# Half a tile of features: both parts of w1 in one stationary operand, and the gate logits on VectorE

## The chip, the core and the metric

The kernel runs on one core of a Trainium2 chip. The metric is the device time of one execution in microseconds, median of several runs. TensorE (PE) multiplies a stationary operand of up to 128 columns with a moving one and adds into PSUM; VectorE (DVE), ScalarE (ACT) and GpSimd (POOL) work element by element; SyncE (SP) issues nearly all transfers between the memories.

## The reference

Two branches of the same input `x` (2048 tokens, 640 features) are mixed by a gate. Branch A is a long convolution over the tokens, whose taps come from a state-space model; branch B is a feed-forward layer with 1728 hidden features.

```python
x = A_u                                               # (1, 2048, 640)
g = sigmoid((x * gate_w).sum(-1, keepdims=True))      # one logit per token
a = conv(x, K) + x * D_skip                           # K: taps, 2048 for each of 640 channels
b = relu(x @ w1) @ w2                                 # w1 (640, 1728), w2 (1728, 640)
return g * a + (1 - g) * b
```

where `K = 2 Re sum_n C[d,n] exp(A[d,n] dt[d] l)` for l = 0 to 2047 (128 terms for each channel).

## The kernel before

**Precision by parts.** Every operand of the feed-forward layer is split into a high part in a rounded 32-bit format (`F32R`) and a low part, the rest: `xh`, `xl` of the tokens, `w1h`, `w1l`, `w2h`, `w2l` of the weights, `hh`, `hl` of the hidden values. A product is the sum of three matmuls, high by high, high by low, low by high. ScalarE makes the high part by a copy, VectorE the low part by a subtraction.

**Tiling.** The 2048 tokens are 8 groups (`g`) of 256. The 1728 hidden features are 13 tiles of 128 and one of 64, the half tile. `PARTS = (5, 5, 4)` deals them to three passes (`p`) over the groups; the half tile is the first of pass 0 (`f = 0`). Its stationary operand has 128 columns: 64 features, then the gate weights as column 64, then zeros. So row 64 of its product is the gate logit of each token.

- `weights` (in `feed_forward`) loads a tile of w1 (`wq` in pass 0, `ws` later) or w2 (`ws`) and splits it.
- `load_x` loads a group's tokens into `xs`, a ring of one buffer. `trans` transposes them on TensorE in three thirds (banks `pk`, `px`, `pg` for group 0, `pk` alone for the others) and splits them into `xh`, `xl`; `store` puts both in `xt`, from which passes 1 and 2 reload them.
- `hidden` makes two tiles of hidden features in one PSUM bank (`pf`, two banks): 3 matmuls of 256 columns for each of 5 blocks `k` of input features and each tile. `high` (ReLU on ScalarE) and `low` (VectorE) make `hh` and `hl` of both. For the half tile, `zc` copies row 64 to `z`, and `zs` stores it to memory.
- `sums` makes the output of a group in four pieces `j` of 128 tokens by 320 columns: 3 matmuls for each hidden tile. In pass 0 ScalarE copies the result to `q`, later passes add with VectorE; `part` holds the sums between passes.
- `gates`, at the start of pass 1, loads all logits and makes `gate` and `omg` (1 - gate) by 17 small VectorE steps.
- `params` computes the parameters of the taps, a chain of VectorE and ScalarE steps on 128 x 640 tiles in the first 80 us, among them an absolute value (`ac`, `as`), reciprocals, arctangent and square root, each of the last two behind a load of ScalarE's tables. The rows that result (`hl` of `split`) are stored to `ps`.
- `ssm` generates the taps in 40 chunks of 16 channels: `load_rows` loads 8 chunks' rows (`PS`, two buffers), `phases` and `exponents` make arguments on TensorE (`pg`, `px`, `pe`), ScalarE makes exponentials and sines, `factors` multiplies on VectorE (`G`, `mg`, `cs`, `sn`), `taps` sums on TensorE (`pk`) and stores to `kd`.
- `conv` is a transform of 64 by 32 points in five blocks of 128 channels: `stage1`, `stage2`, `inv2`, `relay`, `inv1`. Its TensorE work (`pc`) alternates with passes 1 and 2 of the feed-forward layer. The output is mixed as it comes (`with_y`, `with_last`, `inv1`).

**The order.** All these are tasks of a planner (`Plan`): each has an engine, a queue, a duration as its author estimates it, a rank, and what it needs of ring buffers. Tasks of one queue stay in order. When the program is built the planner goes through the time by these estimates and writes a fixed order of instructions for each engine, which the engines then follow. So a change of any duration or dependence can move work between engines everywhere. Generator tasks have a better rank on TensorE than the feed-forward layer's, which fills what they leave.

All instructions go through a helper, so the profile puts nearly all on line 228; groups are told apart by their tiles.

Of the kernel before, what the change touches and what calls it, by code (L numbers as in the profile page):

```python
# [19 lines left out]
NT = D // 128  # L20
# [4 lines left out]
SPIN = 10  # L25

# [223 lines left out]
class Kernel:  # L250
    def __init__(self, tc, ctx, io, out):
# [8 lines left out]
                       xt=[T([2, 128, NT, 256], f"xt{g}") for g in range(8)], z=T([16, 128], "z_"),  # L260
# [17 lines left out]
    def feed_forward(self):  # L278
# [4 lines left out]
        for n, k in dict(ws=3, wq=5, xs=1, xhl=2, q=2, bank=2, z=1).items():  # L283
            ring(n, k)
# [49 lines left out]
        def load_x(g, after=()):  # L334
            s_ = tok('xs')

            def load():
                st['xs', g] = self.xp.tile([128, 2, D], F32, name="xs")
                for h in range(2):
                    D_.dma_start(st['xs', g][64 * h:64 * h + 64], xd[h, :, 2 * g:2 * g + 2, :])  # L340
            return s_, A('SP', 'x', 1.25, load, after, take=[s_], kb=640, rank=2 if g else 0)

        def trans(g, third, src):
# [34 lines left out]
            if third == 2:  # L378
                xst[g] = A('SP', 'st', 1.25, store, X[0, g], use=[x_], kb=1280, rank=6)
# [15 lines left out]

        def hidden(p, g, i, fs):
            b_, h_ = tok('bank'), tok(f"h{i}")

            def pe(r, f, third):
                def go():  # L400
# [3 lines left out]
                    wh, wl = (w.rearrange("p (k f) -> p k f", f=128) for w in (wh, wl))  # L404
                    for k in range(2 * third, min(2 * third + 2, NT)):
                        for m, (a, b) in enumerate(((wh, xh), (wh, xl), (wl, xh))):
                            self.E.matmul(st['hb'][:, r], a[:, k], b[:, k], start=k == m == 0,
                                          stop=k == NT - 1 and m == 2)
                return go
            ts = []  # L410
            for r, f in enumerate(fs):
                (wt, w_) = W[p, f, 0]
                for third in range(3):
                    x = X[p, g] if p else X[p, g][2 * third:2 * third + 2]
                    new = r == third == 0
                    ts.append(A('PE', 'ff', 0.72 if third < 2 else 0.36, pe(r, f, third), [*wt, *x],
                                take=[b_] if new else (), use=[w_, xtok[p, g]] + ([] if new else [b_]), mode='f'))

            if p == 0 and i == 0:
                z_ = tok('z')  # L420

                def zc():
                    st['z'] = pa.tile([65, 256], F32, name="z")
                    V.tensor_copy(st['z'][64:65], st['hb', i][64:65, 0])

                def zs():
                    D_.dma_start(sc['z'][2 * g:2 * g + 2], st['z'][64:65].rearrange("o (t p) -> o t p", t=2))
                zt = A('DVE', 'ff', 0.36, zc, ts, take=[z_], use=[b_], rank=0)
                self.zst.append(A('SP', 'st', 0.62, zs, [zt], use=[z_], kb=2, rank=6))

            def high():
                st['h', i] = [pa.tile([128, len(fs), 256], F32R, name=f"h{x}{i}") for x in 'hl']
                S.activation(st['h', i][0], st['hb', i][:, :len(fs)], AF.Relu)

            def low():
                V.scalar_tensor_tensor(st['h', i][1], st['hb', i][:, :len(fs)], 0.0, st['h', i][0].bitcast(F32),
# [800 lines left out]
```

## Time and profile before

| | |
|---|---|
| median of 3 runs | 714.4 us (713.83 to 715.64) |
| profiled execution: time, span | 717.8 us, 716.0 us |
| mean granted TensorE clock | 0.986 |
| busy: TensorE, VectorE, ScalarE, GpSimd | 679.6, 575.4, 389.2, 72.2 us |
| moved by transfers | 110.84 MB, 155 GB/s |
| first matmul of the generator (`pg`) | 105.08 us |
| first matmul of the convolution (`pc`) | 434.15 us |

A row of a group gives the line, the engine, the operation, output and input tiles, shapes, the count, the busy time, the mean of one in ns, and the idle time before it with what ended it. A row of the timeline gives start and length in us; where rows follow one another they are merged and counted. The chain of waits is followed back from the last instruction.

### The profile page before, as it was taken

The page shows a single profiled execution, that of the slowest core. Times are in us where ns is not written, and L with a number is a line of the kernel's source. Part 1 is how long each engine was busy: PE and PEld are TensorE (multiplying, and loading weights), DVE is VectorE, ACT ScalarE, POOL GpSimd, SP SyncE. Part 2 cuts the span into 40 slices and gives each one's busy share as a digit, 9 for nine tenths or more (in the row PEclk, how much of TensorE's full clock was granted, in tenths as well). Part 3 has the DMA queues.
Part 4 walks back from the last instruction along what each step waited for, and adds up shares of the span by engine and source line. Part 5 has one row for each costly group of instructions (what it writes and reads, how often), then busy time and mean ns, then how long its engine had stood idle before and what let it go on. Part 6 is the DMA issues. An engine that isn't in the chain of part 4 may idle for free.

```text
span 716.0 us, 21643 instructions
## 1 busy us (share of the span) xinstructions
PE 679.6 (95%) x9489; PEld 600.1 (84%) x9489; DVE 575.4 (80%) x833; ACT 389.2 (54%) x572; POOL 72.2 (10%) x81
## 2 busy tenths in 40 slices
PE   5979999999999999999999999989999999899897
PEld 5979998898999999989998897886587776597695
DVE  4499628988999999999999986649869769479675
ACT  4353339999998778787889820151340531241330
POOL 1000002211121221112211100000000000010020
PEclk9899999999999999999999999999999999899999
DMA  9844773254467334423432759924915914731534
GB/s 219 242 193 163 260 240 111 67 179 163 138 199 248 125 124 139 160 88 103 153 108 89 226 166 303 270 93 137 199 44 170 251 56 119 177 97 61 120 98 96
DMA packets 92167, 110.84 MB, mean 155 GB/s; under 512 B 30945, under 2 KB 73705, under 8 KB 91817
## 3 DMA queue, kind: packets, MB, share of 16 engines
q1 hardware_dynamic: 91992, 109.38, 51.9%
q8 instruction: 74, 1.21, 0.7%
q14 instruction: 21, 0.16, 0.1%
q10 hardware_dynamic: 80, 0.08, 0.0%
HBM read 70.24 MB, written 39.20 MB: 153 GB/s over the span
## 4 chain that ended last, share of the span: by engine, by line
PE 69%; DVE 14%; ACT 10%; issue 4%; DMA 2%; SPq 1%; DVEq 0%; ACTq 0%
PE pf L228 40%; PE pc L228 21%; PE pk L228 4%; DVE sn L228 3%; ACT cs L228 3%; DVE G L228 2%; DVE mg L228 2%; ACT sn L228 2%; PE pg L228 2%; ACT L228 1%; PE px L228 1%; DMA xs<-in_A_u_dram 1%; SPq L228 1%; ACT hh L228 1%; DVE cs L228 1%
## 5 line engine op out<-in xcount | busy, mean ns | idle before, releaser
L228 PE MATMUL pf<-xh,w1h 128*128 128x256 f32 x560 | 165.0, 295 | 0.6 <-ACT xh L228 0.6
L228 PE MATMUL pf<-xl,w1h 128*128 128x256 f32 x560 | 159.9, 286 | 0.6 <-DVE xl L228 0.6
L228 PE MATMUL pf<-xh,w1l 128*128 128x256 f32 x560 | 159.5, 285 | 0.0
L228 PE MATMUL pf<-w2h,hh 128*128 128x320 f32 x448 | 140.0, 315 | 2.8 <-DVE hl L228 2.0
L228 PE MATMUL pf<-w2l,hh 128*128 128x320 f32 x448 | 137.6, 310 | 0.0
L228 PEld LDWEIGHTS pf<-xh,w1h 128*128 128x128 f32 x560 | 108.5, 194 | 22.9 <-issue 20.0
L228 PE MATMUL pf<-w2h,hl 128*128 128x320 f32 x448 | 126.4, 311 | 0.5 <-DVE hl L228 0.5
L228 ACT ACTIVATE hh<-pf 128x512 fp32r<-128x512 f32 (+1 forms) x64 | 34.7, 543 | 149.3 <-PE pf L228 142.4
L228 PEld LDWEIGHTS pf<-xl,w1h 128*128 128x128 f32 x560 | 108.5, 194 | 1.8 <-DVE xl L228 0.8
L228 PEld LDWEIGHTS pf<-xh,w1l 128*128 128x128 f32 x560 | 108.5, 194 | 0.0
L228 DVE TENSOR_TENSOR t<-pc,kw 128x512 f32<-128x512 f32 x80 | 53.9, 691 | 50.3 <-ACT kw L228 50.2
L228 PEld LDWEIGHTS pf<-w2h,hh 128*128 128x128 f32 x448 | 84.1, 188 | 11.6 <-issue 5.9
L228 PEld LDWEIGHTS pf<-w2l,hh 128*128 128x128 f32 x448 | 84.2, 188 | 2.4 <-issue 1.6
L228 PEld LDWEIGHTS pf<-w2h,hl 128*128 128x128 f32 x448 | 80.8, 188 | 6.3 <-issue 4.6
L228 POOL TENSOR_TENSOR me<-me,cm 128x512 f32<-128x512 f32 x40 | 51.5, 1287 | 192.7 <-DVE cs L228 115.2
L228 DVE TENSOR_TENSOR mg<-mg,cs 128x1024 f32<-128x1024 f32 x40 | 56.4, 1409 | 1.3
L228 PE MATMUL pc<-va,tm 64*64 64x128 f32 x1280 | 55.3, 277 | 1.9 <-issue 1.9
L228 DVE TENSOR_TENSOR sn<-pg,cs 128x1024 f32<-128x1024 f32 x40 | 48.7, 1216 | 8.6 <-ACT cs L228 8.3
L228 ACT ACT_TABLE_LOAD x42 | 53.9, 1283 | 0.7
L228 ACT CAST cs<-pg 128x1024 int32<-128x1024 f32 x40 | 40.4, 1011 | 20.0 <-PE pg L228 19.8
L228 DVE STREAM_TRANSPOSE vk<-va 128x512 f32<-128x512 f32 x40 | 46.9, 1233 | 4.2 <-ACT va L228 4.2
L228 DVE SCALAR_TENSOR_TENSOR hl<-pf,hh 128x512 fp32r<-128x512 f32 (+1 forms) x64 | 39.3, 616 | 12.3 <-ACT hh L228 11.8
(140 smaller groups left out, 1218.9 us busy)
## 6 DMA issues: line engine op xcount, KB each, us to landing
part<-q SPq DMA_DIRECT2D x16, 640.0 KB, 3.8
xh<-xt SPq DMA_DIRECT2D x16, 640.0 KB, 4.5
xl<-xt SPq DMA_DIRECT2D x16, 640.0 KB, 7.1
q<-part SPq DMA_DIRECT2D x16, 640.0 KB, 4.0
ws<-in_B_w_dram SPq DMA_DIRECT2D x22, 320.0 KB, 3.9
xs<-in_A_u_dram SPq DMA_DIRECT2D x16, 320.0 KB, 4.0
xt<-xh SPq DMA_DIRECT2D x8, 640.0 KB
xt<-xl SPq DMA_DIRECT2D x8, 640.0 KB
```

Of the source, the lines that this page charges most:

```text
L228: return lambda *a, **k: self._tc.keep_in_program_order(f(*a, **k))
```

## The change

In pass 0 the half tile's stationary operand now holds the high part of its 64 features in columns 0 to 63 and the low part in columns 64 to 127. Two matmuls per block, with `xh` and with `xl`, give all the products, in two halves of the PSUM tile that have to be added: ScalarE copies the upper half to `z` (`fold`), VectorE adds the lower one (`total`), ScalarE makes the high part of the hidden values in rows 0 to 63 (`half_high`), VectorE the low part in rows 64 to 127 of the same tile (`half_low`). w2's 64 rows are loaded twice, one copy below the other, so that two matmuls, with `w2h` and `w2l`, do for the three of before.

The gate logits leave TensorE: `gw` holds the gate weights on all 128 partitions, and for each of 16 blocks of 128 tokens one VectorE instruction multiplies `xs` by it in place and adds up the row into `z`, after the group's transposes are through. The next `load_x` waits for both of a group's logits. The logit's way through memory (`zc`, `zs`, the load in `gates`) goes, as do the two memsets. `PS` holds 4 chunks' rows instead of 8. Some names in `conv` get a further index.

```diff
+XS = 1
 ...
+        self.z = keep.tile([128, 16], F32, name="logit")
 ...
         def weights(p, f, two, after=()):
-            first = p == 0 and not two
+            first, half = p == 0 and not two, fn < 128 and not two
 ...
                 if two:
-                    if fn < 128:
-                        P.memset(t[fn:], 0.0)
-                    D_.dma_start(t[:fn], io['B_w2'][f0:f0 + fn, :])
+                    for x in range(0, 128, fn):
+                        D_.dma_start(t[x:x + fn], io['B_w2'][f0:f0 + fn, :])
                     return
                 t = t.rearrange("p (k f) -> p k f", f=128)
-                if fn < 128:
-                    P.memset(t[:, :, fn + 1:], 0.0)
                 D_.dma_start(t[:, :, :fn], io['B_w1'][:, f0:f0 + fn].rearrange("(k p) f -> p k f", p=128))
-                if fn < 128:
-                    D_.dma_start(t[:, :, fn:fn + 1], io['gate_w'].rearrange("(k p o) -> p k o", p=128, o=1))
 ...
             def high():
+                if half:
+                    w, t = (x.rearrange("p (k f) -> p k f", f=128) for x in (st[key][0], st['ws', key]))
+                    S.copy(w[:, :, :fn], t[:, :, :fn])
+                    return
 ...
             def low():
+                if half:
+                    w, t = (x.rearrange("p (k f) -> p k f", f=128) for x in (st[key][0], st.pop(('ws', key))))
+                    V.tensor_sub(w[:, :, fn:], t[:, :, :fn], w[:, :, :fn].bitcast(F32))
+                    return
 ...
+        def logits(g):
+            s_, ld = xs[g]
+
+            def go(t):
+                x = st['xs', g][:, t]
+                V.scalar_tensor_tensor(x, x, 1.0, self.gw, op0=ALU.mult, op1=ALU.mult,
+                                       accum_out=self.z[:, 2 * g + t:2 * g + t + 1])
+            for t in range(2):
+                self.zs.append(A('DVE', 'z', 0.75, lambda t=t: go(t), [*self.x_read[-3:], self.gwl], use=[s_], rank=0))
 ...
         def hidden(p, g, i, fs):
+                    ms = ((wh, xh), (wh, xl), (wl, xh))[:2 if halves(p, f) else 3]
 ...
+            n = len(fs) - halves(p, fs[0])
+            lo = len(fs) - n
+
+            def fold():
+                st['z'] = pa.tile([64, 256], F32, name="z")
+                S.copy(st['z'], st['hb', i][64:, 0])
+
+            def total():
+                V.tensor_add(st['z'], st['hb', i][:64, 0], st['z'])
 ...
+            def half_high():
+                S.activation(st['h', i][0][:64, 0], st['z'], AF.Relu)
+
+            def half_low():
+                h = st['h', i][0][:, 0]
+                V.scalar_tensor_tensor(h[64:], st['z'], 0.0, h[:64].bitcast(F32), op0=ALU.max, op1=ALU.subtract)
 ...
+                x = A('ACT', 'ff', 0.32, fold, ts, take=[z_], use=[b_], rank=0)
+                x = A('DVE', 'ff', 0.35, total, [x], use=[b_, z_], rank=0)
+                x = A('ACT', 'ff', 0.32, half_high, [x, a], use=[z_, h_], rank=0)
+                x = A('DVE', 'ff', 0.35, half_low, [x], use=[z_, h_], rank=0)
 ...
         def sums(p, g, j, q_, qld):
-            prod = [(f, *x) for f in range(n) for x in ((0, 0), (0, 1), (1, 0))]
+            prod = [(f, *x) for f in range(n) for x in ((0, 0), (0, 1), (1, 0))[:2 if halves(p, f) else 3]]
 ...
+        def load_gate():
+            D_.dma_start(self.gw, io['gate_w'].rearrange("(o d) -> o d", o=1).to_broadcast([128, D]))
         xs = {0: load_x(0)}
         W[0, 0, 0] = weights(0, 0, 0)
+        self.gwl = A('SP', 'w', 0.62, load_gate, kb=320, rank=1)
 ...
         def load_rows(c):
-                t = gk.tile([128, 8, 128], F32R, name="PS", bufs=2)
-                src = self.sc['ps'][c > 0][c // 8 - 1 if c else 0]
+                t = gk.tile([128, 4, 128], F32R, name="PS", bufs=2)
+                src = self.sc['ps'][c >= 8][c // 8 - (c >= 8), c % 8 * C:c % 8 * C + 4 * C]
```

More of the change, by code (lines that the diff above doesn't have):

```diff
@@ L415, in hidden @@
                     new = r == third == 0
-                    ts.append(A('PE', 'ff', 0.72 if third < 2 else 0.36, pe(r, f, third), [*wt, *x],
+                    ts.append(A('PE', 'ff', (0.72 if third < 2 else 0.36) * (2 / 3 if halves(p, f) else 1), pe(r, f, third), [*wt, *x],
                                 take=[b_] if new else (), use=[w_, xtok[p, g]] + ([] if new else [b_]), mode='f'))
[L419 to L429, printed above, removed]
+            n = len(fs) - halves(p, fs[0])
@@ new lines, in half_high @@
+            def half_high():
[3 more added lines that the diff above has]
+                V.scalar_tensor_tensor(h[64:], st['z'], 0.0, h[:64].bitcast(F32), op0=ALU.max, op1=ALU.subtract)
+            a = A('ACT', 'ff', 0.12 + 0.2 * n, high, ts, take=[h_], use=[b_], rank=0)
+            b = A('DVE', 'ff', 0.08 + 0.27 * n, low, [a], use=[b_, h_], rank=0)
+            H[p, g, i] = [(a, b)] * len(fs), h_
@@ L540, in go @@
                 V.tensor_mul(self.omg, z, self.gate)
-            a = A('SP', 'q', 0.62, load, self.zst, kb=8, rank=3)
-            rec = Recorder(V)
+            rec, a = Recorder(V), self.zs
             for k in range(17):
-                a = A('DVE', 'gate', 0.2, rec.one(k, 17, go), [a], rank=4)
-            self.gated = a
-        self.zst, self.x_read = [], []
+                a = [A('DVE', 'gate', 0.2, rec.one(k, 17, go), a, rank=4)]
+            self.gated = a[0]
+        self.zs, self.x_read = [], []
         def spin():
```

70 lines of the change are left out of this document (36 added, 34 removed).

## The prediction

> **What bounds the kernel now.** I read the page's busy shares and chain first, then the busy times in three stretches, then the rows around each wait of TensorE.
>
> ```profile
> PE 679.6 (95%) x9489; PEld 600.1 (84%) x9489; DVE 575.4 (80%) x833; ACT 389.2 (54%) x572; POOL 72.2 (10%) x81
> ...
> PE 69%; DVE 14%; ACT 10%; issue 4%; DMA 2%; SPq 1%; DVEq 0%; ACTq 0%
> ```
>
> TensorE is busy for 95% of the span and carries 69% of the chain, so work taken from it counts unless something else comes last in its place. The three stretches (core's PE, PEld, DVE, ACT, POOL busy, clock, DMA share, GB/s) are: before the generator of the convolution taps starts, the generator, and the convolution.
>
> ```profile
> 0.00:105.00 105.00, 91.76 (x655) 90.44 (x656) 64.25 (x120) 39.36 (x72) 1.81 (x9) 0.95 0.74 224
> 105.00:434.00 329.00, 320.81 (x4479) 301.43 (x4477) 303.55 (x420) 271.68 (x325) 60.22 (x60) 1.00 0.45 144
> 434.00:716.00 282.00, 267.07 (x4360) 208.21 (x4358) 207.64 (x293) 78.20 (x176) 10.15 (x12) 0.98 0.54 142
> ```
>
> TensorE idles 13.2 us in the first stretch, 8.2 in the second, 14.9 in the third. VectorE is loose first (40.8 idle), but in the second it is nearly as full as TensorE (25.4 idle of 329). So the change exchanges TensorE time against VectorE time where VectorE has least to spare.
>
> **What leaves TensorE.** A row of a matmul shows its length with the pipeline in it; the cost is the spacing, which two pieces of the chain show: 15 hidden matmuls of 256 columns, and 60 output matmuls of 320.
>
> ```profile
> 89.63 1.79 PE pf L228 x15
> 91.70 8.81 PE pf L228 x60
> ```
>
> That is 0.119 us and 0.147 us each. In the half tile each of 8 token groups loses 5 hidden matmuls (three per k become two, five k) and 4 output matmuls (three products become two in each of four sums). The built instruction order agrees: 1680 hidden and 1344 output matmuls become 1640 and 1312. 40 x 0.119 + 32 x 0.147 = 9.5 us. That the change doesn't do what it says is thereby ruled out. The Trainium skill (TensorE: Matmul & The Clock Gate, Back-to-back issue gap) gives an isolated warm gap of N/2.4 + 2.5 ns; by it the removed work would be an estimated 8.7 us. The trace's spacings are some 10 ns wider than that, and they decide.
>
> **What VectorE and ScalarE get.**
>
> ```profile
> L228 DVE SCALAR_TENSOR_TENSOR sa<-sa,ra 128x640 f32<-128x640 f32 x6 | 4.9, 820 | 0.1
> L228 DVE SCALAR_TENSOR_TENSOR hl<-pf,hh 128x512 fp32r<-128x512 f32 x48 | 32.8, 683 | 10.8 <-ACT hh L228 10.3
> L228 DVE SCALAR_TENSOR_TENSOR hl<-pf,hh 128x256 fp32r<-128x256 f32 x16 | 6.6, 415 | 1.4 <-ACT hh L228 1.4
> L228 DVE TENSOR_TENSOR xl<-pk,xh 128x256 fp32r<-128x256 f32 x7 | 2.9, 412 | 0.0
> L228 DVE COPY z<-pf 1x256 f32<-1x256 f32 x8 | 3.4, 422 | 16.6 <-PE pf L228 15.0 <-ACT hh L228 1.6
> L228 ACT ACTIVATE hh<-pf 128x512 fp32r<-128x512 f32 x48 | 28.6, 596 | 142.7 <-PE pf L228 135.8 <-DVE z L228 6.8
> L228 ACT ACTIVATE hh<-pf 128x256 fp32r<-128x256 f32 x16 | 6.1, 383 | 6.6 <-PE pf L228 6.6
> ```
>
> Per group VectorE gains two logits (0.82 each: the 128x640 instruction of the same kind), the add of the two halves (0.41) and the low part of the half (0.42); it loses the copy of the logit row (0.42) and half of one low part (0.27): +1.78, or 14.2 us over 8 groups. No row has a logit's accumulating output: 0.82 is the lower bound, two passes (1.64) the upper; I take 0.82, since two full-width f32 inputs already cost no more in that row. ScalarE gains two 64x256 steps (0.38 each) and loses 0.21: +0.55 per group, 4.4 us, in 327 us of its own idle time. Five groups' VectorE work lies at least partly ahead of 105 us, where it is loose; three groups (5.3 us) fall into the full stretch.
>
> The removed logit transfers, the two memsets on GpSimd and the smaller gate load had nobody waiting long; the row loads become ten of half the size, each buffer still freed four chunks (some 33 us, 329/40 x 4) before its next use: nothing for all of these.
>
> **First wait: the second token load.** Its buffer is the only one, and the logits now hold it longer.
>
> ```profile
> 9.06 1.11 SPq L228 DMA_DIRECT2D xs<-in_A_u_dram  x2
> 10.05 0.41 DVE L228 TENSOR_TENSOR xl<-pg,xh 128x256 fp32r<-128x256 f32 x1
> 17.99 1.08 PE L228 MATMUL pk<-ident,xs 128*128 128x128 f32 x4 [4.67 <-DMA xs<-in_A_u_dram]
> ...
> xs<-in_A_u_dram SPq DMA_DIRECT2D x16, 320.0 KB, 4.0
> ```
>
> The load was issued at 9.06, as soon as the transposes were through. In the new order both logits stand behind the last xl; its weight step is 0.4 shorter, so they end near 10.05 + 2 x 0.82 = 11.7. The load then lands between 11.7 + 0.6 + 4.0 = 16.3 (the usual landing) and 11.7 + 8.9 = 20.6 (as slowly as now, where weights share the queue). Ahead of it on SP there are now 480 KB more (gate weights on all partitions, the half's w2 twice), 2.2 us at 224 GB/s, against a column load that goes. I take 1.3 us later (0 to 2.7). The first group's five hidden matmuls lie ahead of this wait, so their 0.6 us brings nothing.
>
> **Second wait: the parameter chain.**
>
> ```profile
> 32.09 0.74 ACT L228 ACTIVATE ac<-ld_A_C_real 128x640 f32<-128x640 f32 x1
> 33.49 0.83 DVE L228 TENSOR_TENSOR mx<-ac,as 128x640 f32<-128x640 f32 x1 [3.48 <-ACT as L228]
> 33.97 0.43 ACT L228 COPY q<-pf 128x320 f32<-128x320 f32 x1 [0.51 <-PE pf L228]
> 39.72 0.82 DVE L228 TENSOR_TENSOR r<-mn,s 128x640 f32<-128x640 f32 x1
> 47.87 0.63 DVE L228 TENSOR_TENSOR xl<-pk,xh 128x512 fp32r<-128x512 f32 x1
> 48.55 1.12 PE L228 MATMUL pk<-ident,xs 128*128 128x128 f32 x4 [4.80 <-DVE xl L228]
> ```
>
> TensorE waits here for xl, which stands behind ScalarE's arctan steps. In the new order `ac` comes after the third q copy, not the second: 34.40 + 1.3 - 3 x 0.147 = 35.3, and with the 1.4 from ac to mx, mx starts near 36.6, 3.1 late. Up to r, VectorE has three steps of the half tile more (1.24): r ends near 44.9 instead of 40.54. Then arctan and square (1.5), with one table load less ahead of xh than before, and seven of the chain's VectorE steps: xl ends near 49.5, 1.05 later than now. Without it TensorE would come here 0.1 late (1.3 less the 0.59 of four output and 0.6 of five hidden matmuls). The wait grows by 0.95 (0 to 2).
>
> **Four smaller costs, behind that.**
>
> ```profile
> 85.00 0.60 PE L228 MATMUL pk<-ident,xs 128*128 128x128 f32 x4
> 86.95 0.68 DVE L228 TENSOR_TENSOR xl<-pk,xh 128x512 fp32r<-128x512 f32 x1
> 89.03 0.60 PE L228 MATMUL pk<-ident,xs 128*128 128x128 f32 x4
> ```
>
> *The transpose bank.* xl is through at 87.63, and TensorE wants the bank at 89.03: 1.4 us of slack. Now xh queues behind the half's second ScalarE step, which needs the fold, the add and their order in one PSUM bank: about 0.8 longer, more with a chain step of 0.8 between. 0 to 0.5 in each of six groups: 0.7 in sum (0 to 3).
>
> ```profile
> 80.87 0.82 DVE L228 TENSOR_TENSOR hl<-ld_A_log_A_real,hl 128x640 fp32r<-128x640 f32 x1
> 82.75 5.75 SPq L228 DMA_DIRECT2D ps<-hl  x6
> 94.05 2.73 SPq L228 DMA_DIRECT2D PS<-ps  x2
> 105.08 0.63 PE L228 MATMUL pg<-tg,PS 128*128 128x512 f32 x2
> ```
>
> *The generator's start.* The chain's last VectorE step, at 81.7, comes up to 3.1 + 1.2 + 4 x 0.82 = 7.6 us later, less what goes into its own waits: some 6. The six stores, issued by 88.5, then end near 95, and behind a token load and two stores of x the row loads are issued near 98. TensorE now gets there at 105.1 + 1.05 - 3.5 (what groups 1 to 4 save after the wait) = 102.6, and 98 + 4 to 6 is when the rows land: 0.6 (0 to 3).
>
> *VectorE in the generator.* 5.3 us go into 25.4 of idle time. TensorE always has hidden and output work to go on with there, but in a fixed order: 0.7 (0 to 5.3).
>
> *The convolution.* Behind its first instruction the new order has 399 hidden and 336 output matmuls instead of 420 and 338. These 2.8 us of filling are missing in two of its five blocks, and TensorE already idles 14.9 us there: 0.9 of it isn't gained (0 to 2.8).
>
> **The sum.** -9.5 + 0.6 + 1.3 + 0.95 = -6.65, then + 0.7 + 0.6 + 0.7 + 0.9 = -3.75. The profiled execution took 717.8 us (span 716.0, 1.8 around it), 3.4 above the median of 714.4; the difference is carried over: 717.8 - 3.75 = 714.05 there, **710.7 in the median**. Its own range is 708 to 713.
>
> **Rivals.** A measurement tells this kernel from no change at about 0.3%, 2.1 us: faster is under 712.3, slower over 716.5.
>
> *All is gained* (0.16): the four smaller costs and the second wait come to nothing: -9.5 + 0.6 + 1.3 = -7.6, 706.8. For it: TensorE idles only 8.2 us of 329 although VectorE is nearly full. Against: the new chain of four steps per group.
>
> *Eaten up* (0.17): the four costs are twice what I took: -6.65 + 5.8 = -0.85, 713.6.
>
> *VectorE sets the pace* (0.14, slower): the generator ends when VectorE is through; the convolution then takes its 282 us whatever filling is left; TensorE's saving becomes idle time. With the row loads no earlier than now, the end moves by the 5.3 us of three groups: 719.7. It decides once the stretch's VectorE idle time is of waits that can't be filled. For it: 303.6 busy of 329. Against: the new order puts fewer matmuls ahead of the convolution (1241 and 976 against 1260 and 1006, 6.7 us by the spacings above).
>
> *The logits run two passes* (0.08, slower): 1.64 each. The token load is later by 1.0, the chain by 3.3, of which 3.0 reach the generator's start, and half of 6 x 0.82 there: -3.75 + 1.0 + 3.0 + 2.4 = +2.65, 717.1. The Trainium skill (Vector Engine (DVE) Microarchitecture Reference, 7. Points that are easy to get wrong) says that this kind of instruction with two sources that aren't bf16 runs at half throughput, no port being left to read the accumulator back. The 820 ns row, as long as plain two-input steps, doesn't show it, but it has no accumulator.
>
> That a later token load is waited for is unlikely and not priced:
>
> ```profile
> 91.73 1.12 SPq L228 DMA_DIRECT2D xs<-in_A_u_dram  x2
> 103.93 0.60 PE L228 MATMUL pk<-ident,xs 128*128 128x128 f32 x4
> ```
>
> 11 us from issue to use less 1.1 + 4.0 leaves 7; two logits and a step before them take 2.5.
>
> **Chances.** The forecast has 0.45, of which 0.04 lie within 0.3%. Faster: 0.41 + 0.16 = 0.57; same: 0.04 + 0.17 = 0.21; slower: 0.14 + 0.08 = 0.22. The range goes from 705.5 (all gained, and the token load on time: 706.8 - 1.3) to 718.5 (past the two-pass case, and most of the way to the pace rival's 719.7, since part of its 5.3 us would be hidden); it leaves out the rest of that rival and the case of all four bounds at their worst.
>
> **What would show it.** Right: 80 hidden-half matmuls where 120 stood; the token wait of 4.67 us near 6, the xl wait of 4.80 near 5.7; the logit rows near 0.82; the first pg near 103; the convolution's first matmul some 2 to 4 us ahead of 434; PE idle in the middle stretch under 10 us. Wrong: a logit over 1 us, a generator that ends after 434, repeated waits of transposes for xl, or more than 18 us of TensorE idle time behind 434.

## The result, and the profile after

The changed kernel took 721.8 us in the median of 6 runs (717.8 to 724.3), the kernel before on the same chip 714.6; the ratio is 1.0098 (95% interval 1.0073 to 1.0123). By this ratio it is slower by 0.98%, 7.0 us, where 3.75 less were forecast. The profiled execution took 724.3 us (span 722.1), 2.5 above its median, as that of before was 3.4 above its own. Below, percentages are against the kernel before in runs of the same chip (its medians there are 714.8 to 716.3); 1% is 7.15 us. The changed kernel itself was timed in the runs above alone, and its 0.98% is carried over to the other chips.

The busy shares of the page after, then its busy times in the same three stretches (columns as before):

```profile
PE 673.4 (93%) x9417; PEld 593.2 (82%) x9417; DVE 588.1 (81%) x873; ACT 394.3 (55%) x588; POOL 71.5 (10%) x79
```

```profile
0.00:105.00 105.00, 87.78 (x614) 85.75 (x615) 71.65 (x145) 42.27 (x81) 0.87 (x7) 0.93 0.73 219
105.00:438.00 333.00, 321.64 (x4470) 300.89 (x4469) 309.06 (x438) 273.81 (x331) 60.40 (x60) 0.99 0.44 146
438.00:722.00 284.00, 264.01 (x4337) 206.59 (x4336) 207.38 (x292) 78.21 (x176) 10.18 (x12) 0.97 0.54 140
```

TensorE's busy time fell by 6.2 us. It is not 9.5, since the granted clock is lower in all three stretches (0.93, 0.99, 0.97 against 0.95, 1.00, 0.98); a kernel below with the same matmuls, the half tile alone, has the mean clock of before, 0.986, and 667.8 us busy. Its idle time rose from 13.2 to 17.2, from 8.2 to 11.4 and from 14.9 to 20.0: 12.3 us more. That is 6.1 net, the difference of the spans. What the change took from TensorE came back as waiting, twice over, and in every stretch.

The waits of TensorE in the head (timeline after; in brackets the idle time and what ended it):

```profile
11.95 0.39 PE L229 MATMUL pf<-xh,w1l 128*128 128x256 f32 x1 [1.31 <-DVE w1l L229]
20.41 1.09 PE L229 MATMUL pk<-ident,xs 128*128 128x128 f32 x4 [6.66 <-DMA xs<-in_A_u_dram]
49.96 1.12 PE L229 MATMUL pk<-ident,xs 128*128 128x128 f32 x4 [5.88 <-DVE xl L229]
105.06 0.62 PE L229 MATMUL pg<-tg,PS 128*128 128x512 f32 x2
438.15 1.95 PE L229 MATMUL pc<-ck,tf 64*64 64x512 f32 x16
```

The first wait is 2.0 longer than before, the second 1.1, and a new one of 1.3 stands in front. With them the generator starts at 105.06, exactly where it started before, although 25 hidden and 16 output matmuls fewer lie ahead of it; the convolution starts 4.1 later.

The logits on VectorE (timeline): the first one, in the head, and one in the generator with the GpSimd step beside it:

```profile
9.59 0.81 DVE L229 SCALAR_TENSOR_TENSOR xs<-xs,gw 128x640 f32<-128x640 f32 x1
10.33 0.08 DVE L229 DVE_READ_ACCUMULATOR xs<-xs,gw 128x1 f32 x1
```

```profile
170.89 1.50 POOL L229 TENSOR_TENSOR me<-me,cm 128x512 f32<-128x512 f32 x1
171.40 1.67 DVE L229 SCALAR_TENSOR_TENSOR xs<-xs,gw 128x640 f32<-128x640 f32 x1
```

One pass of 0.81 and a read of the accumulator of 0.08, no two passes. Of the 16 logits 14 take 0.81 to 0.83; the two others take 1.32 and 1.67.

What TensorE's convolution work (`pc`) waits for (total, times, longest), after and then before:

```profile
PE pc L229 <- issue: 7.2, 7, 3.0
PE pc L229 <- DVE t L229: 4.1, 4, 1.3
PE pc L229 <- DVE yj L229: 1.8, 3, 0.8
PE pc L229 <- ACT yj L229: 1.0, 1, 1.0
```

```profile
PE pc L228 <- issue: 4.6, 5, 2.4
PE pc L228 <- DVE t L228: 2.8, 3, 1.3
PE pc L228 <- DVE yj L228: 1.4, 2, 0.8
PE pc L228 <- ACT va L228: 0.7, 1, 0.7
```

With one more of 0.4 in both, and without the rows of "issue" (waiting for nothing that the profile shows), these are 7.3 us after and 5.3 before. The rows of "issue" differ by 2.6, but they range from 3.7 to 7.4 in kernels that have the convolution of before, so this difference isn't shown to be the change's. The timeline shows where the difference lies, at the start of the fourth block, first after, then before:

```profile
619.31 0.45 PE L229 MATMUL pc<-vk,tm 64*64 64x128 f32 x8 [1.27 <-DVE t L229]
621.47 0.55 PE L229 MATMUL pc<-vk,tm 64*64 64x128 f32 x8 [1.27 <-DVE t L229]
624.13 0.71 PE L229 MATMUL pc<-vk,tm 64*64 64x128 f32 x8 [1.25 <-DVE t L229]
```

```profile
618.63 0.45 PE L228 MATMUL pc<-vk,tm 64*64 64x128 f32 x8 [1.27 <-DVE t L228]
620.73 1.48 PE L228 MATMUL pc<-t,tn 64*64 64x128 f32 x32 [1.22 <-DVE t L228]
622.90 0.70 PE L228 MATMUL pc<-vk,tm 64*64 64x128 f32 x8 [0.69 <-ACT va L228]
```

Each step of this block goes TensorE, ScalarE, VectorE and back. Where feed-forward matmuls stand between, nobody sees it; after the change the last ones are used up a step or two earlier.

### The profile page after: what moved, and what is told of

It reads as the page before. It is cut to its first block, busy times and chain, and to the rows that moved or that the text cites. A ratio compares the mean times of both kernels' runs of the same rounds, so it can differ in the third digit from the quotient of the medians.

```text
span 722.1 us, 21565 instructions
## 1 busy us (share of the span) xinstructions
PE 673.4 (93%) x9417; PEld 593.2 (82%) x9417; DVE 588.1 (81%) x873; ACT 394.3 (55%) x588; POOL 71.5 (10%) x79
## 5 line engine op out<-in xcount | busy, mean ns | idle before, releaser
L229 PE MATMUL pf<-xh,w1h 128*128 128x256 f32 x560 | 161.7, 291 | 0.0
L229 PE MATMUL pf<-xl,w1h 128*128 128x256 f32 x560 | 158.2, 285 | 0.3 <-DVE xl L229 0.3
L229 PE MATMUL pf<-xh,w1l 128*128 128x256 f32 x520 | 148.2, 285 | 1.3 <-DVE w1l L229 1.3
L229 PE MATMUL pf<-w2h,hl 128*128 128x320 f32 x416 | 118.0, 313 | 0.7 <-DVE hl L229 0.7
L229 ACT ACTIVATE hh<-pf 128x512 fp32r<-128x512 f32 (+1 forms) x64 | 33.0, 516 | 143.6 <-PE pf L229 143.4
L229 PEld LDWEIGHTS pf<-xh,w1l 128*128 128x128 f32 x520 | 100.8, 194 | 1.5 <-DVE w1l L229 1.5
L229 PEld LDWEIGHTS pf<-w2h,hl 128*128 128x128 f32 x416 | 74.9, 188 | 9.6 <-issue 7.5
L229 DVE TENSOR_TENSOR mg<-mg,cs 128x1024 f32<-128x1024 f32 x40 | 58.4, 1461 | 1.2
L229 PE MATMUL pc<-t,tn 64*64 64x128 f32 x1280 | 49.4, 279 | 6.8 <-issue 5.6
L229 DVE SCALAR_TENSOR_TENSOR hl<-pf,hh 128x512 fp32r<-128x512 f32 (+1 forms) x64 | 37.1, 580 | 22.8 <-ACT hh L229 12.1
```

Source lines behind the costliest of these rows:

```text
L229: return lambda *a, **k: self._tc.keep_in_program_order(f(*a, **k))
```

## The experiments

### What the saving is worth, and what is paid for it

**The 72 matmuls put back into the changed kernel.** Same order of instructions on every engine, same added steps.

```diff
+                    if halves(p, f) and third == 0:
+                        for k in range(NT):
+                            self.E.matmul(st['hb'][:, r], wh[:, k], xh[:, 0], start=True, stop=True)
 ...                 # and one output product more in each of four sums
```

> The changed kernel with 72 matmuls put back at the places where it saves them (5 hidden and 4 output products more in each token group, whose results are overwritten): the order on all engines is that of the changed kernel, word for word. If the removed work is worth its length in the changed kernel too: 7 to 9.5 us more than the changed kernel, 727 to 731. If most of it would lie in waits that are there anyway (the second load, xl behind the parameter chain, the generator's VectorE steps): 2 to 5 us more, or less still, since the idle time no longer halves the clock: 720 to 726.

728.3 us, +1.98% (1.74 to 2.23). Against the changed kernel's 0.98% that is 1.0% or 7.1 us (4.6 to 9.7 from both intervals). So at its own place the removed work is worth most of its 9.5 us, and this kernel, with all that the change adds and nothing that it saves, shows the price in this order: 1.98%, 14.2 us. Its busy times by stretch (head, chunks 1 to 16 of the generator, the rest of it, convolution), and the two middle ones of before:

```profile
0.00:110.00 110.00, 91.50 (x656) 89.99 (x657) 71.74 (x144) 42.15 (x81) 0.87 (x7) 0.94 0.71 214
110.00:234.00 124.00, 116.22 (x1483) 108.45 (x1482) 112.94 (x168) 108.40 (x144) 21.56 (x21) 1.00 0.48 157
234.00:447.00 213.00, 208.06 (x3023) 195.13 (x3025) 197.27 (x271) 165.18 (x187) 38.56 (x39) 1.00 0.42 135
447.00:729.00 282.00, 261.77 (x4335) 203.99 (x4327) 207.36 (x292) 78.30 (x176) 10.21 (x12) 0.99 0.53 140
```

```profile
105.00:217.00 112.00, 108.47 (x1426) 101.05 (x1425) 101.15 (x132) 104.80 (x135) 22.34 (x21) 1.00 0.45 142
217.00:434.00 217.00, 212.34 (x3055) 200.39 (x3054) 202.39 (x289) 166.88 (x191) 37.87 (x39) 1.00 0.45 145
```

TensorE's idle time is 18.5, 7.8, 4.9 and 20.2 here, 13.2, 3.5, 4.7 and 14.9 before: the price is 15.1 us of waiting, a third each in the head, in the first chunks of the generator and in the convolution. In the first chunks the largest part is waits for `kt`, here and then before (total, times, longest):

```profile
PE pk L229 <- DVE kt L229: 2.4, 2, 2.1
```

```profile
PE pk L228 <- DVE kt L228: 0.5, 1, 0.5
```

These are single profiles, and the last third is the least certain: behind the first `pc` TensorE idles 14.9 to 18.8 us in the profiles with the convolution of before, and 17.3 to 20.2 in those with the changed one. No run has the added steps in the old order, so how much of the price is the steps' own time, and how much the new order, stays open.

**The same 72 left out of the kernel before,** with nothing added and its order kept.

```diff
+                        ms = ((wh, xh), (wh, xl), (wl, xh))[:2 if parts[p][f][1] < 128 else 3]
 ...
+                        if parts[p][f][1] < 128 and x:
+                            continue
```

> The kernel before with the 72 matmuls left out that the change removes (the product of the half tile's low weights with the tokens, and in each output sum the product of its low activations; so a part of the half tile's precision is left out), with no other instruction added, moved or dropped: the order on the other engines is that of before, word for word. It prices the saving alone. If TensorE's time counts there as the prediction's sum took it, 9.5 less the 0.6 ahead of the first wait: 7 to 9 us less than before, 706 to 709. If the waits of the head and the VectorE chain in the generator set the pace behind them, TensorE's saving turns into idle time: 2 to 5 us less, 710 to 713. Order theory: the whole 7 to 9 us, and what the changed kernel loses beside it comes from the new order and the added steps.

713.5 us, -0.11% (-0.34 to 0.11): 0.8 us less (2.4 less to 0.8 more). That is less than any theory had. In an order that was laid out for these matmuls, their absence is nearly all waited out. The profile shows where. The generator starts at 100.71 instead of 105.08, so 4.4 of the 5.3 us left out ahead of it are gained; it then takes 329.6 us, against 329.0, so nothing of the 4.1 us left out in it is; and the convolution, in which nothing is left out, takes 1.9 longer, with 2.8 more of "issue". The experiments on VectorE, below, take this up.

### Logits or half tile

**The changed kernel without its logit instructions** (the logits stay zero; the gate weights are still loaded).

```diff
-            for t in range(2):
-                self.zs.append(A('DVE', 'z', 0.75, lambda t=t: go(t), ...))
+            return
```

> The changed kernel with the sixteen logit instructions left out (all logits are zero; the gate weights are still loaded): the half tile alone. The token buffer is free again after the transposes. Theory 1 (the logits on VectorE carry the loss, by holding the token buffer and by VectorE time in the generator): 705 to 709 us, the 9.5 us of TensorE less some 2. Theory 2 (the half tile's chain of four steps over two engines carries it): 715 to 720. Theory 3 (small idle times throw TensorE's clock to half for stretches of 3.4 us, whichever part makes them): the time follows the sum of half-clock time, 30.7 us in the changed kernel and 20.4 in the kernel before; below 714 only if that sum is at or under 20.

719.1 us, +0.43% (0.20 to 0.66): the half tile by itself is still a loss, as the second theory had it.

**The logits alone:** the half tile as before, three matmuls and zeros, but the logits on VectorE and row loads of four chunks.

```diff
-            first, half = p == 0 and not two, fn < 128 and not two
+            first, half = p == 0 and not two, False
 ...
         def halves(p, f):
-            return parts[p][f][1] < 128
+            return 0
```

> The kernel before with the logits on VectorE alone: the half tile keeps its three matmuls per block (zeros in the other columns), row loads in halves as in the changed kernel. Nothing leaves TensorE. Theory 1: 5 to 9 us slower than before, 720 to 724. Theory 2: within 3 us of before, 714 to 717. Theory 3: slower by half of whatever half-clock time is added, plus the idle time.

722.9 us, +1.05% (0.78 to 1.32): the logits by themselves are one too, as the first theory had it, and as large a one as the whole change.

**The half tile alone, nothing of the logits:** no instruction, no gate weights, row loads of eight chunks.

```diff
-        self.gwl = A('SP', 'w', 0.62, load_gate, kb=320, rank=1)
 ...
-                t = gk.tile([128, 4, 128], F32R, name="PS", bufs=2)
+                t = gk.tile([128, 8, 128], F32R, name="PS", bufs=2)
```

> The half tile alone: the changed kernel without logits, without the load of the gate weights and with row loads of eight chunks as before (the gate's logits are left at zero). Against the run without logits only, it drops the 320 KB on the queue and the halved row loads. If the logits' load and the smaller row loads set the rest of its loss: 709 to 712, the half tile is then a gain. If the four-step chain of the half tile and its new order lose what it saves: 715 to 719, and the convolution's idle time is again near 15 us, with 399 hidden matmuls in it instead of 420.

716.9 us, +0.28% (0.13 to 0.44). So the half tile costs 2.0 us net, and the logits with all that is theirs the other 0.70% (0.41 to 0.99), 5 us. The two parts don't add up, though: 0.28% and the 1.05% of the logits alone are 1.33%, more than the 0.98% of the change, and with the logits there (1.05%) the half tile costs nothing more. The convolution's idle time is 19.2 us in this run, where near 15 was expected. The issue of the second token load on SP's queue and the head's waits, first of this kernel, then the loads of the one without instructions only, then those of the changed kernel with its second logit:

```profile
9.44 1.11 SPq L229 DMA_DIRECT2D xs<-in_A_u_dram  x2
17.79 1.09 PE L229 MATMUL pk<-ident,xs 128*128 128x128 f32 x4 [5.65 <-DMA xs<-in_A_u_dram]
47.61 1.11 PE L229 MATMUL pk<-ident,xs 128*128 128x128 f32 x4 [5.88 <-DVE xl L229]
```

```profile
8.51 2.73 SPq L229 DMA_DIRECT2D ws<-in_B_w_dram  x4
11.37 1.11 SPq L229 DMA_DIRECT2D xs<-in_A_u_dram  x2
```

```profile
7.89 2.72 SPq L229 DMA_DIRECT2D ws<-in_B_w_dram  x4
11.07 0.08 DVE L229 DVE_READ_ACCUMULATOR xs<-xs,gw 128x1 f32 x1
11.24 1.11 SPq L229 DMA_DIRECT2D xs<-in_A_u_dram  x2
```

Without the gate weights the token load is issued at 9.44, near the 9.06 of before. With them the issues ahead of it on SP end at 11.24 where no logit holds the buffer, and at 10.61 in the changed kernel, where the second logit then ends at 11.15. So the 320 KB of gate weights cost this load 1.2 to 1.8 us, and the hold came last in the changed kernel, but only by half a microsecond. The second wait is 5.88 with and without logits, and 3.72 in the run with the logits alone: that one is the half tile's.

**Row loads of four chunks, nothing else.**

> The kernel before with row loads of four chunks instead of eight, as the change has them, and nothing else; TensorE's and VectorE's order stay the same. As the prediction had it they cost nothing: within 2 us of before. If the halved loads, ten in place of five on SP's queue, are a good part of the change's price: 3 us and more above before.

714.8 us, +0.04% (-0.19 to 0.28). They cost nothing, as forecast.

**Logits of 16 columns** instead of 640, in the changed kernel's order.

```diff
-                x = st['xs', g][:, t]
-                V.scalar_tensor_tensor(x, x, 1.0, self.gw, op0=ALU.mult, op1=ALU.mult,
+                x = st['xs', g][:, t, :16]
+                V.scalar_tensor_tensor(x, x, 1.0, self.gw[:, :16], op0=ALU.mult, op1=ALU.mult,
```

> The changed kernel with its 16 logit instructions on 16 columns instead of 640 (the logits are then wrong): the order and all loads are those of the changed kernel, and 16 x 0.7 us of VectorE time are gone. If the logits' VectorE time is what they cost: 3 to 5 us less than the changed kernel, 717 to 719, as without them. If their place in the order, the token buffer that they hold or the load of the gate weights is: within 1.5 us of the changed kernel, 720 to 723.

719.5 us, +0.74% (0.54 to 0.93), 0.24% less than the changed kernel (0.08 more to 0.56 less), between the two expectations. So of the logits' 0.70% their VectorE time is perhaps 0.24%. Leaving the instructions out altogether took off 0.55% (0.98 to 0.43), so some 0.3% would be their place in the order; the 0.15% between that run and the half tile alone (0.43 to 0.28) would be the load of the gate weights and the smaller row loads. Neither the 0.24% nor the 0.15% is clear of nothing by itself.

### The two waits of the head

Three edits: the transposes of groups 1 to 3 through three banks instead of one; a buffer of its own for the second token group, loaded early; both; and both in the kernel before.

```diff
-            bank = ('pk', 'px', 'pg')[0 if g else third]
+            bank = ('pk', 'px', 'pg')[third if g < 4 else 0]
 ...
+                own = self.prm.tile([128, 2, D], F32, name="xs1") if g == 1 else None
```

> The changed kernel, but the transposes of token groups 1 to 3 go through three PSUM banks (pk, px, pg in turn) as those of group 0 do, instead of through pk alone, so that TensorE need not wait for xl to free the one bank. Waits theory: the second wait (5.9 us for the first third, 1.3 to 3 us for the next) goes in good part, and with it some of the half-clock time behind it; 3 to 7 us less than the changed kernel, 715 to 719. Generator theory (the loss lies in the four-step chain and the logits beside the generator): the generator starts earlier but its chunks 1 to 16 still take 119 to 121 us instead of 112, and the convolution's idle time stays near 20 us. Rival: the wait only moves, because the weights of group 1's first matmul need xl all the same; then within 2 us of the changed kernel.

> The changed kernel, but the second token group has a buffer of its own, and its load is put on the queue ahead of the second-layer weights instead of behind the first group's release. Waits theory: the first wait (6.7 us) shrinks to under 2 us, the stretch of half clock behind it may go too: 3 to 7 us less than the changed kernel, 715 to 719. Rival: what bounds the first 20 us is the bytes on the queue, and the later weights are then waited for instead: within 2 us of the changed kernel. The generator's loss (119 to 121 us for its chunks 1 to 16) should not change.

> The changed kernel with both: three banks and the second token group's own early buffer. If the two waits at the head and the half clock behind them are all that the change lost, it gains what the kernel before with the same two edits gains less 9.5 us of matmuls, and is faster than that one. If the loss lies in the generator and the convolution (theories of the four-step chain and of the logits), it stays 3 to 7 us slower than the kernel before with the same two edits: 713 to 716.

> The kernel before with the same two edits (three banks for the transposes of groups 1 to 3, and a buffer of its own and an early load for the second token group). It has waits of 4.7 and 4.8 us there and about 10 us of half clock in the first 60 us; with both waits gone TensorE reaches the generator up to 9 us earlier, if the generator's rows are there by then; 707 to 711. If the rows are not, 711 to 714, and TensorE waits for the rows near 100 us instead.

Banks: 720.9 us, +0.67% (0.43 to 0.92). Own buffer: 725.8, +1.37% (0.87 to 1.86). Both: 726.3, +1.47% (0.99 to 1.95). Both in the kernel before: 713.4, -0.23% (-0.46 to 0.00). The timeline with the early load:

```profile
17.31 0.63 PE L229 MATMUL pk<-ident,xs 128*128 128x128 f32 x4 [1.58 <-DMA xs<-in_A_u_dram]
50.40 1.12 PE L229 MATMUL pk<-ident,xs 128*128 128x128 f32 x4 [7.90 <-DVE xl L229]
```

The first wait shrank from 6.66 to 1.58, and the second took it over: TensorE goes on at 50.40, as at 49.96. With three banks the second wait goes, but one of 3.9 us for `hl` takes its place, the planner puts more feed-forward work ahead and the first `pg` comes at 111.92 (both: 115.17). The expectation of 3 to 7 us for each wait fell; the one that the loss lies elsewhere stood, and more: with both edits in both kernels the change costs 1.7% (1.0147 against 0.9977), not 1.0%.

### The clock

Idle matmuls in the two waits of the head: 28 and 24 in the changed kernel, 18 and 19 in the one before; then there also 5 in each of two waits of the convolution's fourth block; then these 10 with banks and own buffer.

```diff
+        def fill(k):
+            def go():
+                p = self.psg.tile([128, 16, 32], F32, name="pe").rearrange("p a b -> p (a b)")
+                for _ in range(k):
+                    self.E.matmul(p[:, :128], self.ident, self.ident, start=True, stop=True)
+            A('PE', 'ff', 0.0, go, mode='f')
```

> The changed kernel with 28 idle matmuls in TensorE's wait for the second token load and 24 in the wait for xl near 44 us, short of the waits, all other instructions in the same order. Theory 3: the half-clock stretches after both waits (13.6 us, 6.8 us lost) go or shrink: 3 to 6 us less than the changed kernel, 716 to 719, and less spread. Theories 1 and 2: no change beyond 1 us, since the same waits stay.

> The kernel before with 18 and 19 idle matmuls in the same two waits. Theory 3: its half-clock stretches there (10.2 us, 5.1 lost) go or shrink: 2 to 5 us less, 710 to 712. Theories 1 and 2: no change beyond 1 us.

> The kernel before with idle matmuls in the two waits of the head (as in the earlier run) and five more in each of two waits of 1.27 us at the start of the convolution's fourth block, near 617 us. Half-clock theory: the stretch of half clock at 621 us goes too; up to 3 us less than with the two waits of the head alone: 711 to 713. Rival: half clock isn't set off by these waits, or the block is bound by VectorE: no difference from 713.7.

> The kernel before with three banks for the transposes of groups 1 to 3, a buffer of its own and an early load for the second token group, and five idle matmuls in each of two waits of the convolution's fourth block. Waits theory: as the same two edits without the idle matmuls, 0.2% to 0.4% faster than before, 711 to 714. If the half clock near 621 us matters beside that: another 1 to 2 us. If idle matmuls there cost what they save, as the last run of that kind had it: no better than 713.

Changed kernel: 720.0 us, +0.51% (0.28 to 0.74), against 0.98% without. Before: 713.7, -0.43% (-0.63 to -0.23). Both are above what was expected of the clock (716 to 719, 710 to 712). Before with ten more: 715.7, +0.18% (-0.01 to 0.37). With banks and own buffer: 715.2, +0.11% (-0.14 to 0.36). The granted clock in 40 slices (tenths, 9 is full) of the changed kernel, of it with idle matmuls in the head, and of the kernel before with them; then the busy times of the one with ten more, right behind these:

```profile
PEclk9889999999999999999999999999999999799999
```

```profile
PEclk9999999999999999999999999999999999799999
```

```profile
PEclk9999999999999999999999999999999999999999
```

```profile
620.00:624.50 4.50, 3.81 (x76) 3.41 (x80) 1.10 (x2) 2.79 (x9) 0.00 (x0) 0.62 0.28 62
```

In the head the idle matmuls do hold the clock up; the ten in the convolution don't, the clock is 0.62 behind them. That the full clock in the head gives time is shown in one set of runs and not in the next, on a kernel that differs by ten idle matmuls in waits; two effects of 0.2% to 0.4% with opposite signs can't be told apart here, the less so as the kernel before itself took 716.3 us on the chip of the first two and 714.8 on that of the third. So none of these versions is shown to beat the kernel before for good, and none of the changed ones comes near it.

### VectorE in the generator

One VectorE step of the generator (`mg`, 1.41 us) cut to half its columns in 20 of 40 chunks: in the kernel before, in it without the 72 matmuls, and in the changed kernel.

```diff
+                        if c < 20:
+                            m = m[:, :, :1]
-                        V.tensor_mul(m, m, cs[:, :, None, 32:].to_broadcast([128, C, 2, 32]))
+                        V.tensor_mul(m, m, cs[:, :, None, 32:].to_broadcast([128, C, 1 if c < 20 else 2, 32]))
```

> The kernel before with the same cut of the VectorE step alone. VectorE as a pace setter beside TensorE: 3 to 8 us less, 707 to 712. If TensorE's work alone sets the pace there (97% busy from 105 to 434 us): within 2 us of before, 713 to 717.

> The kernel before without the 72 matmuls, and with one VectorE step of the generator (1.41 us over 1024 columns) cut to half its columns in the first 20 of 40 chunks (their taps are then wrong): about 0.7 us less VectorE time in each, 14 us in sum, in the same order on every engine. If VectorE, or the engines' turns together, eat TensorE's saving in the generator: the two cuts together bring clearly more than each alone, 7 us or more below the same cut without the 72 left out, 700 to 706. If TensorE's saving is lost elsewhere (the two waits of the head, the clock, the convolution): within 3 us of the same cut without them.

> The changed kernel with one VectorE step of the generator (1.41 us over 1024 columns) cut to half its columns in the first 20 of 40 chunks (their taps are then wrong), in the changed kernel's own order. The same cut brought 0.15% (-0.06 to 0.37) to the kernel before. If the changed kernel loses in the generator because VectorE is over-full there: it brings 0.7% or more here, 5 us and up, 713 to 717. If its loss is in the head and the convolution and in the order: as little as before, 719 to 722.

VectorE's busy time falls by 10 us (575.4 to 565.3 in the kernel before), not by the 14 expected. Before: 713.6 us, -0.15% (-0.37 to 0.06). With the 72 left out too: 710.4, -0.57% (-0.78 to -0.37). Changed kernel: 719.5, +0.79% (0.47 to 1.11), 0.2% less than without the cut. The first matmul of the convolution in the kernel before (its generator starts at 105.08), then the first of the generator and of the convolution without the 72, with the cut, with both:

```profile
434.08 1.95 PE L228 MATMUL pc<-ck,tf 64*64 64x512 f32 x16
```

```profile
100.71 0.63 PE L228 MATMUL pg<-tg,PS 128*128 128x512 f32 x2
430.36 1.95 PE L228 MATMUL pc<-ck,tf 64*64 64x512 f32 x16
```

```profile
105.56 0.63 PE L228 MATMUL pg<-tg,PS 128*128 128x512 f32 x2
431.23 1.95 PE L228 MATMUL pc<-ck,tf 64*64 64x512 f32 x16
```

```profile
99.92 0.63 PE L228 MATMUL pg<-tg,PS 128*128 128x512 f32 x2
424.19 1.95 PE L228 MATMUL pc<-ck,tf 64*64 64x512 f32 x16
```

Alone, 9.5 us of TensorE bring 3.7 up to the convolution and 10 us of VectorE 2.9; together they bring 9.9, 3.3 more than the sum. But 1.3 of these 3.3 lie ahead of the generator, where nothing of VectorE is cut: profiles of one order differ there (105.08 and 105.56, 100.71 and 99.92). The generator itself takes 329.0, 329.6, 325.7 and 324.3 us. So without the 72 nothing is gained in it, with the cut 3.3, and with both 4.7: 1.4 of the 4.1 us of matmuls left out there come out once VectorE has room. In the whole times the two together bring 0.57%, the sum of the two is 0.26%, and the difference of 0.31% has an uncertainty of 0.37%. Engines that eat up each other's gain were expected to show 7 us or more below the cut alone; it is 3.0 (0.9 to 5.1), the most that the other expectation allowed. So that two engines in step each hide a part of what the other gains is suggested by these runs and not shown. The convolution, the same in all four, takes 281.9, 283.8, 280.0 and 284.5 us; what its "issue" waits are stays open. In the changed kernel the cut brings no more than in the one before, where 0.7% or more was expected of an over-full VectorE in the generator; so that is not borne out as what the change pays for.

## Why the prediction was wrong

**What bounds the kernel.** "TensorE is busy for 95% of the span ... so work taken from it counts unless something else comes last in its place": in the order of before something else comes last for most of it (9.5 us out, 0.8 gained; in the generator 4.1 out and nothing gained).

**The saving.** -9.5 + 0.6 = -8.9 was forecast; at the changed kernel's order it is 7.1 (4.6 to 9.7). Count and spacing were right (1640 hidden and 1312 output matmuls in the trace), the size about so.

**The price is the step that failed:** 1.3 + 0.95 + 0.7 + 0.6 + 0.7 + 0.9 = 5.15 us were set against the saving, 14.2 (12.4 to 15.9) were paid in the changed order. Taken the other way round, with the saving at its 0.8 in the old order, the rest is 7.8 (5.4 to 10.2). So the terms of the sum depend on each other, but either way the added steps and the order that comes with them cost more than 5.15.

- *First wait,* 1.3 (0 to 2.7): the transposes came 2.4 later. The load was issued at 11.24 (forecast 11.7) and waited for until 20.41, 9.2 later, as slow as the upper bound had it (8.9). Of the two causes named the bytes ahead on SP weigh more, and the hold by the logits adds at most half a microsecond. Who else waits behind these bytes was left out: `w1l`, 1.31.
- *Second wait,* 0.95: TensorE goes on at 49.96 after 5.88 us (forecast: xl ends near 49.5, wait near 5.7). Right, and the half tile's steps are the cause.
- *Generator's start:* 103 forecast, 105.06 measured. The rows were not late; the waits above and the clock ate all of the 5.3 us (25 x 0.119 + 16 x 0.147) saved ahead of it.
- *Transposes and VectorE in the generator,* 0.7 each: the transposes' waits for `xl` in chunks 1 to 16 are 0.7 us after and 1.1 before, so that term came to nothing. Yet idle time there is 4.3 more with the matmuls put back. Of it 1.9 are waits for `kt`, which VectorE makes behind two steps of the generator itself, and 1.5 one "issue" wait. It is not shown to be VectorE's fill (9 us less there bring 0.2%, the logits' own time 0.24%), and no run shows which part of the new order makes it.
- *The convolution,* 0.9 (0 to 2.8): idle time +5.1, of it 2.0 in waits that the profile can name. They are the same in the changed kernel, without logits and with narrow ones: it is the order, with 399 and 336 feed-forward matmuls left instead of 420 and 338. The logits alone, which save nothing, leave 399 and 336 too; so the lost filling isn't the saved work, as the prediction took it, but what the planner made of new steps. Another 2.6 us are "issue", within what these waits differ by in one and the same convolution.
- *The logit:* 0.81 and 0.08, near the lower bound taken; two passes are out. Two of the 16 were over the mark of 1 us that was set, both beside a GpSimd step.

**The rivals.** "VectorE sets the pace" came nearest with 719.7 and was right that the saving would become idle time and the convolution would take its time whatever filling is left (284 us against 282). Its mechanism, a VectorE too full in the generator, is not borne out by the cuts, so its time was near by luck.

**The range** ended at 718.5 because it left out "the case of all four bounds at their worst". The terms were ranged one by one as if independent; but all came from one new fixed order in which several engines are full, and most went up together (the first wait, the generator's start and its idle time, the convolution). By their upper ends the sum would have been 2.7 + 2 + 3 + 3 + 5.3 + 2.8 - 8.9 = 9.9 above before; 7.0 were measured.

## What to carry to other kernels

In a kernel with a fixed order in which TensorE, VectorE and ScalarE are all over 90% busy (108.5, 101.2 and 104.8 of the 112 us from 105 on, before), work taken from one engine need not be worth its length: here 9.5 us out of TensorE brought 0.8 (2.4 less to 0.8 more) in the old order, while the same work put back cost 7.1 in the new one. Price an added step by every wait that it may lengthen behind it in its queue, and take these prices as moving together. The two probes that show it are cheap: leave the saved work out of the old kernel without the new steps, and put it back into the new one.

## What the runs showed of the hardware

**Short waits close together can halve TensorE's clock.** The busy times of before around 618 to 628 us, then those of the run with row loads of four chunks behind the same waits:

```profile
618.00:622.00 4.00, 2.15 (x56) 1.73 (x56) 1.58 (x4) 0.37 (x1) 0.00 (x0) 0.92 0.27 79
622.00:628.00 6.00, 5.32 (x96) 4.71 (x96) 1.68 (x4) 3.01 (x10) 0.00 (x0) 0.50 0.45 113
```

```profile
620.50:626.00 5.50, 4.29 (x148) 4.05 (x152) 2.24 (x5) 3.97 (x12) 0.00 (x0) 1.00 0.53 128
```

No wait there is longer than 1.27 us, yet in before the clock is at 0.50 for the 6 us behind them, in which TensorE is busy. In the other run the waits are the same and the clock stays full, so they can do it but need not. The Trainium skill (TensorE: Matmul & The Clock Gate, HAM oscillation) puts the rule as no idle gaps over some 3.4 us; these rows show that gaps of 1.2 us in a row can do it too, which is nearer to that page's account of a monitor that looks at windows of activity.

**A multiply with a row sum is one pass.** It takes 0.81 us and 0.08 for reading the sum, where 0.82 is what the plain step of that width with two f32 sources took. With one source it is 0.49:

```profile
L228 DVE TENSOR_SCALAR r<-ph 128x640 f32<-128x640 f32 x2 | 1.0, 488 | 0.0
```

The Trainium skill (Vector Engine (DVE) Microarchitecture Reference, 7. Points that are easy to get wrong) has half throughput for two sources that aren't bf16. The trace agrees if that is meant against one source, 0.82 to 0.49; the row sum doesn't halve it once more.

**A VectorE step can take twice as long beside a GpSimd step.** The two logits of 1.32 and 1.67 us are the ones that ran while GpSimd was at its `me` step, in the changed kernel and again with the 72 matmuls put back. In the run with the logits alone none met one, and all 16 took 0.81 to 0.83.
